# The second expert's first product made by seven quarter products, with the sums for it ordered among the first expert's work

## The chip, the cores and the metric

The kernel runs on one core of a Trainium2 chip. The time is that of the device, in microseconds (us), of one execution; the kernel before was executed three times. The profile is one further look at such an execution, with every instruction's start and duration. TensorE is called PE in it, VectorE DVE, ScalarE ACT, GpSimd POOL, and SP is the engine whose queue issues nearly all transfers here.

## The reference

Causal attention with a forgetting bias, then a mixture of 8 experts whose weights come from a Sinkhorn normalisation over all tokens, then a bilinear layer. There are 1152 tokens (2 x 576) of width 512; an expert is 512 to 1024 to 512.

```python
attn = softmax(q @ k.T / 8 + min(-(cum_i - cum_j), 0), causal)   # 2 batches, 8 heads, 576 x 64
x = (attn @ v) as (1152, 512)
P = exp(x @ w_gate - max)
for _ in range(8):                       # Sinkhorn
    P /= P.sum(1, keepdims=True) + 1e-9
    P /= P.sum(0, keepdims=True) + 1e-9
    P *= 1152 / 8
out = sum_e P[:, e:e+1] * (relu(x @ w1[e]) @ w2[e])
return (out @ w_a) * (out @ w_b) @ w_out
```

## The kernel before

Each float32 matrix is held as two float16 parts, a high one (`hi_of`, on ACT) and the remainder (`lo_of`, on DVE), and each product is three PE products (high x high, high x low, low x high). Weights arrive in `stage` buffers of 1 MB, their scale is found (`sumsq` on ACT, a maximum over partitions, `pow2` on DVE), and `split` writes the two parts into `wun` buffers. Nine token tiles `t` = 0 to 8 go through attention; tile 8 holds the last 64 tokens of both batches.

The program is not written in its final order. Every piece of work is an entry of a graph (`g.add`, with an engine, a cost, keys that it reads and writes, and a rank), and `emit` makes the order of each engine by list scheduling with the costs of the entries. It does so in two parts: entries ahead of the mark `g.cut` are planned and re-ranked first, those behind it are planned after that, on engines that are already taken up to the end of the first part. So on every engine all of the first part stands ahead of all of the second.

The first part is attention and, tile by tile, the gate and expert 0 (`e0_tile`: gate product, two `h_quad` of 48 matmuls with 128 columns, then 24 matmuls with 512 columns into `mb`, L1041 to L1043). `switch` closes the attention buffers and opens those of the experts (`ht`, `sx`, `ts`, `mr`) once all tiles of `xt`, the transposed input of the experts, are there. The last entry of the first part is `w_prep(1, 1, ...)`, load, scale and split of expert 1's `w1`.

The second part begins with `sinkhorn()`: a maximum of the logits (L1144), a transpose and a broadcast on PE (L508, L510), an exponential on ACT (L1148), eight rounds of four DVE operations over rows (L1151 to L1154), one PE product with ones (L1168) and five DVE operations over columns (L1160 to L1164), then nine scalings of `acc` (L1176). Expert 1's first product is `h_plain`: three blocks of 384 tokens, eight columns of weights, 12 matmuls each (L998 to L1000), one eviction by ACT (L1003) and one by DVE (L1004). Experts 2 to 7 use `h_seven`: both factors are cut into quarters, seven products of sums of quarters replace eight, in matmuls of 288 columns (L1393 to L1395), with additions on DVE (L1408), copies on ACT (L1412) and the evictions L1403 and L1404. For it `x_sums` makes four sums of quarters of x once (28 additions on DVE at L1317, eight copies on ACT at L1321, rank 202.5, behind `w_prep(2, 1, ...)`), and `w_sums` makes the sums of the weights for each expert (four subtractions L1351, seven pairs of L358 on ACT and L372 on DVE). All experts end with `y_tile`: per token tile 24 matmuls with 512 columns (L1041 to L1043) into one of two `yb` banks and an eviction into `acc` (L1451).

Of the kernel before, what the change touches and what calls it, by code (L numbers as in the profile page):

```python
# [11 lines left out]
F16 = mybir.dt.float16  # L12
# [40 lines left out]
class Graph:  # L53
# [179 lines left out]
    def emit(self):  # L233
        self.begin()
        self.stale = True
        for seed in SEEDS:
            self.rerank(seed)
        state = self.schedule(0, self.cut)
        order = self.order
        self.schedule(self.cut, None, state)  # L240
        for t, i, k in order + self.order:
            fn = self.ops[i][2]
            (fn[k] if isinstance(fn, tuple) else fn)()
# [3 lines left out]
def forgetting_attention_moe_bilinear_kernel(  # L247
# [22 lines left out]
    KF = FF // 128  # L270
# [3 lines left out]
    NB = NTL // BT  # L274
    BN = BT * 128
# [8 lines left out]
    g = Graph()  # L284
# [18 lines left out]
    stage = [const.tile([128, 2048], F32, name=f"stage{i}") for i in range(2)]  # L303
    units = [const.tile([128, 2, 4, 512], F16, name=f"wun{i}") for i in range(4)]
# [4 lines left out]
    CN = HT // 2  # L309
# [99 lines left out]
    st = [aps.tile([128, 512], F32, name=f"st{i}") for i in range(NST)]  # L409
# [12 lines left out]
    def mbk(m):  # L422
# [11 lines left out]
          w=["clamp"], rank=0)  # L434
# [525 lines left out]
    def frank():  # L960
        fr[0] += 1
        return 1e4 + fr[0]
# [131 lines left out]
    yb = []  # L1094

    def switch():
        att.close()
        bp = ctx.enter_context(tc.tile_pool(name="big", bufs=1))
        for i in range(4, 7):
            units.append(bp.tile([128, 2, 4, 512], F16, name=f"wun{i}"))  # L1100
        big["ht"] = bp.tile([128, 2, KF, NT], F16, name="ht")
        big["sx"] = bp.tile([128, 4, 2, 2, HT], F16, name="sx")
        big["jk"] = bp.tile([128, 1024], F16, name="jk")
        big["mr"] = bp.tile([128, 2048], F32, name="mr")
        for i in range(2):
            big["ts", i] = bp.tile([128, 1024], F32, name=f"ts{i}")
            big["s5", i] = bp.tile([128, CN], F32, name=f"s5_{i}")
            big["w", i] = bp.tile([128, CN], F32, name=f"w22_{i}")
            big["o", i] = big["ts", i][:, 0:DM]
        stage.append(big["mr"])  # L1110
        for i in range(2):
            units.append(stage[i].bitcast(F16).rearrange("p (z c f) -> p z c f", z=2, c=4))
        big["g0"] = big["sx"].rearrange("p i z c t -> p (i z c t)").rearrange("p (z f t) -> p z f t", z=2, f=4)
        yp = ctx.enter_context(tc.tile_pool(name="ps_y", bufs=1, space=PSUM))
        mb.append(yp.tile([128, 512], F32, name="mb2"))
        for i in range(5):
            yb.append(yp.tile([128, 512], F32, name=f"yb{i}"))
# [4 lines left out]
    def hk(z, f, c0=0, c1=NT):  # L1122
# [1 line left out]

    allh = [x for z in range(2) for f in range(KF) for x in hk(z, f)]
    sxk = [("sx", i, z, c) for i in range(4) for z in range(2) for c in range(2)]
    bigk = ([("u", i, z, c) for i in range(4, 7) for z in range(2) for c in range(4)] + [("yb", i) for i in range(5)] + allh + sxk
            + [("o", i) for i in range(2)] + [("a", i) for i in range(2)] + [("s5", i) for i in range(2)] + [("w", i) for i in range(2)]
            + [("st", 2, c) for c in range(4)] + mbk(2) + ["switch"])
    g.add("-", 0, switch, r=attk, w=bigk)  # L1130
# [157 lines left out]
    def h_cols(c0, c1):  # L1288
        return (lambda z, f: big["ht"][:, z, f, c0:c1]), (lambda z, f: hk(z, f, c0, c1))

    def h_plain(e):

        for b in range(NB):
            dst, dkey = h_cols(b * BN, (b + 1) * BN)
            for f in range(KF):
                h_item(e, b * BN, BN, f, dst, dkey)

    def slot(i):
        return (0, 1, 4, 5)[i // 2], 2 * (i % 2)

    def slot_keys(i):
        u, c0 = slot(i)
        return [("u", u, z, c) for z in range(2) for c in (c0, c0 + 1)]

    quad = lambda z, r, t: xt[:, z, 2 * r:2 * r + 2, t * HT:(t + 1) * HT]

    def x_sums():

        rk = 202.5
        sk, uk = [("o", 0), ("a", 0)], [("o", 1), ("a", 1)]  # L1310
        xk = [("xt", t) for t in range(NTL)]
        for c in range(2):
# [28 lines left out]
    def w_sums(e, rank):  # L1341
# [9 lines left out]
            g.add("DVE", 1280, lambda: nc.vector.tensor_tensor(out=out(), in0=a(), in1=b(), op=ALU.subtract), r=r, w=w, rank=rank)  # L1351

        def split(i, src, keys):
            u, c0 = slot(i)
            part = [lambda y=y: units[u][:, y, c0:c0 + 2].rearrange("p c f -> p (c f)") for y in range(2)]
            k = [[("u", u, y, c) for c in (c0, c0 + 1)] for y in range(2)]
            g.add("ACT", 1144, lambda: hi_of(part[0](), src(), sx), r=keys + [("ws", 1, e)], w=k[0], rank=rank)
            g.add("DVE", 1290, lambda: lo_of(nc.vector, part[1](), src(), sx, part[0]()), r=keys + [("ws", 1, e)] + k[0], w=k[1], rank=rank)
# [15 lines left out]
    def h_seven(e):  # L1374
# [7 lines left out]

        def prod(i, j, c, bank, bk, first):
            src, keys, wi = ops[i]
            u, ch0 = slot(wi)

            def mm():
                p = bank()[:, 0:CN]
# [5 lines left out]
                    nc.tensor.matmul(p, lhsT=wh, rhs=xl, start=False, stop=False, skip_group_check=True)  # L1394
                    nc.tensor.matmul(p, lhsT=wl, rhs=xh, start=False, stop=ch == 1, skip_group_check=True)  # L1395

            g.add("PE", 6 * (CN / 2.4 + 2.7), mm, r=keys + slot_keys(wi), w=bk, rank=frank())

        def out(src, bk, f, s_, c):
            c0 = s_ * HT + c * CN  # L1400
# [279 lines left out]
                    m2_prep(wi, pc, 6, prank())  # L1680
                m2_out(wi, x, prank())

    w_prep(1, 1, (4, 5), 150, fine=True, rel=REL_E1)()
    g.cut = len(g.ops)
    early[0] = False
    dense[0] = True
    sinkhorn()
    g.add("PE", 700, set_bits, r=[("xt", t) for t in range(NTL)], w=[("yb", i) for i in range(2, 5)], rank=frank())
    for e in range(1, E):
        last = e == E - 1  # L1690
        if e == 1:
            h_plain(e)
        else:
            h_seven(e)
        w_prep(2, e, (2, 3), prank())()
        if e == 1:
            x_sums()
        if not last:
            w_prep(1, e + 1, (None, None), prank())
        g.add("-", 0, lambda: None, r=hk(0, 0), w=["hold"])  # L1700
# [78 lines left out]
```

## Time and profile before

| what | value |
|---|---|
| executions | 1064.58, 1064.61, 1066.53 us; median 1064.61 |
| span of the profiled execution | 1065.9 us |
| PE busy | 1009.7 us, 95% of the span |
| DVE busy | 716.6 us, 67% |
| ACT busy | 514.8 us, 48% |
| POOL busy | 156.9 us, 15% |
| mean granted PE clock | 0.992 of 2.4 GHz |

The profile gives no time of its own for the profiled execution beside the span from its first to its last instruction; that span is 1.3 us above the median of the three executions. A matmul's duration in it overlaps the next one's, so the spacing of starts is what a matmul costs. DVE and ACT durations overlap by some 0.1 us likewise.

### The profile page before, as it was taken

How to read it: one execution, taken by the hardware profiler on the slowest of the kernel's cores; microseconds unless marked ns; L12 is line 12 of the kernel's file. 1: busy time of each engine (PE TensorE's matmuls, PEld its weight loads, DVE VectorE, ACT ScalarE, POOL GpSimd, SP SyncE). 2: the span in 40 equal slices, each digit the busy share in tenths (PEclk: the TensorE clock that was granted, in tenths of full speed). 3: DMA queues.
4: the chain of work that ended last, by engine and by line, in shares of the span. 5: the costliest groups of instructions: out<-in, count | busy, mean ns of one | idle time of the engine just before them, and what ended most of it. 6: DMA issues, size and time to landing. Idle time of an engine off the chain costs nothing.

```text
span 1065.9 us, 19044 instructions
## 1 busy us (share of the span) xinstructions
PE 1009.7 (95%) x7739; PEld 626.9 (59%) x7739; DVE 716.6 (67%) x1490; ACT 514.8 (48%) x966; POOL 156.9 (15%) x192
## 2 busy tenths in 40 slices
PE   1498999999999999999999999999999999999998
PEld 0476877765546754764774575476477464555445
DVE  7885674149975898796699879578768785444201
ACT  4587477246534644753662664356444344443100
POOL 3977576120000000000000000000000000000000
PEclk9899999999999999999999999999999999999999
DMA  9893951002223125423323340341443652310001
GB/s 240 161 195 78 173 81 23 2 15 76 79 80 117 43 104 173 159 80 119 119 80 121 147 168 41 120 155 43 158 158 110 207 129 79 119 40 1 21 30 40
DMA packets 123063, 108.75 MB, mean 102 GB/s; under 512 B 87632, under 2 KB 100176, under 8 KB 119136
## 3 DMA queue, kind: packets, MB, share of 16 engines
q1 hardware_dynamic: 121920, 107.27, 34.3%
q8 instruction: 60, 0.98, 0.4%
q10 hardware_dynamic: 1056, 0.28, 0.1%
q14 instruction: 27, 0.22, 0.1%
HBM read 75.29 MB, written 18.09 MB: 88 GB/s over the span
## 4 chain that ended last, share of the span: by engine, by line
PE 88%; DVE 6%; DMA 2%; issue 1%; POOL 1%; ACT 1%; SPq 0%; DVEq 0%; POOLq 0%; ACTq 0%
PE yb L1041 10%; PE yb L1042 10%; PE yb L1043 10%; PE yb L1393 4%; PE yb L1395 4%; PE yb L1394 4%; PE mb L1393 3%; PE mb L1394 3%; PE mb L1395 3%; PE yb L1647 2%; PE yb L1648 2%; PE yb L1649 2%; PE yb L1578 2%; PE yb L1579 2%; PE yb L1577 2%; DVE wun L372 2%
## 5 line engine op out<-in xcount | busy, mean ns | idle before, releaser
L1041 PE MATMUL yb<-wun,ht 128*128 128x512 f16 x504 | 191.1, 379 | 0.0
L1042 PE MATMUL yb<-wun,ht 128*128 128x512 f16 x504 | 191.1, 379 | 0.0
L1043 PE MATMUL yb<-wun,ht 128*128 128x512 f16 x504 | 191.1, 379 | 0.0
L372 DVE SCALAR_TENSOR_TENSOR wun<-stage,sc,wun 128x1024 f16<-128x1024 f32 (+1 forms) x66 | 79.7, 1231 | 11.5 <-ACT wun L358 11.5
L1043 PEld LDWEIGHTS <-ht 128*128 128x128 f16 x504 | 49.3, 98 | 59.5
L1393 PE MATMUL yb<-sx,wun 128*128 128x288 f16 x288 | 82.4, 286 | 2.0 <-DVE sc L343 1.1
L1451 DVE SCALAR_TENSOR_TENSOR acc<-yb,pe,acc 128x512 f32<-128x512 f32 x63 | 47.3, 750 | 54.1 <-PE yb L1043 53.1
L1042 PEld LDWEIGHTS <-ht 128*128 128x128 f16 x504 | 49.3, 98 | 57.7 <-issue 0.3
L1041 PEld LDWEIGHTS <-ht 128*128 128x128 f16 x504 | 49.3, 98 | 57.6
L1395 PE MATMUL yb<-sx,wun 128*128 128x288 f16 x288 | 82.4, 286 | 0.0
L1394 PE MATMUL yb<-sx,wun 128*128 128x288 f16 x288 | 82.4, 286 | 0.0
L1394 PEld LDWEIGHTS <-wun 128*128 128x128 f16 x672 | 65.7, 98 | 24.7 <-issue 6.2
L1393 PEld LDWEIGHTS <-wun 128*128 128x128 f16 x672 | 65.7, 98 | 18.4
L1395 PEld LDWEIGHTS <-wun 128*128 128x128 f16 x672 | 65.7, 98 | 16.6
L358 ACT ACTIVATE wun<-stage,sc 128x1024 f16<-128x1024 f32 (+1 forms) x58 | 59.7, 1052 | 29.8 <-DVE sc L343 14.7
L355 ACT ACTIVATE jk<-stage 128x1024 f16<-128x1024 f32 x52 | 54.7, 1052 | 37.5 <-DMA stage<-in_moe_w_dram 37.1
L897 POOL TENSOR_TENSOR pt<-p,pt 128x512 f16<-128x512 f32 (+1 forms) x46 | 55.0, 1198 | 25.3 <-ACT pt L894 19.4
L1403 ACT ACTIVATE ht<-yb 128x288 f16<-128x288 f32 x96 | 38.8, 406 | 40.7 <-PE yb L1395 40.1
L1393 PE MATMUL mb<-xt,wun 128*128 128x288 f16 x192 | 55.0, 286 | 0.0
L1394 PE MATMUL mb<-xt,wun 128*128 128x288 f16 x192 | 55.0, 286 | 0.0
L1395 PE MATMUL mb<-xt,wun 128*128 128x288 f16 x192 | 54.9, 286 | 0.0
L1404 DVE SCALAR_TENSOR_TENSOR ht<-yb,ht 128x288 f16<-128x288 f32 x96 | 43.0, 453 | 17.2 <-ACT ht L1403 16.9
(355 smaller groups left out, 2641.8 us busy)
## 6 DMA issues: line engine op xcount, KB each, us to landing
stage<-in_moe_w_dram SPq DMA_DIRECT2D x26, 1024.0 KB, 5.5
md<-wun SPq DMA_DIRECT2D x15, 1024.0 KB, 3.8
wun<-md SPq DMA_DIRECT2D x11, 1024.0 KB, 5.4
stage<-in_moe_w_dram SPq DMA_DIRECT2D x24, 256.0 KB, 3.9
mr<-in_moe_w_a_dram SPq DMA_DIRECT2D x12, 512.0 KB, 6.0
mr<-in_moe_w_b_dram SPq DMA_DIRECT2D x12, 512.0 KB, 4.0
mr<-in_moe_w_out_dram SPq DMA_DIRECT2D x6, 1024.0 KB, 5.4
stage<-md SPq DMA_DIRECT2D x4, 1024.0 KB, 4.8
```

The lines of the kernel that those rows point to most:

```text
L355: nc.scalar.activation(out, src, AF.Square, accum_out=dst)
L358: nc.scalar.activation(hi, src, AF.Copy, scale=scale)
L372: eng.scalar_tensor_tensor(out=lo, in0=src, scalar=scale, in1=hi, op0=ALU.mult, op1=ALU.subtract)
L897: lambda hi=hi, lo=lo, src=src: nc.gpsimd.tensor_tensor(out=lo, in0=src, in1=hi, op=ALU.subtract)),
L1041: nc.tensor.matmul(pp, lhsT=hh, rhs=wh, start=(f == 0), stop=False)
L1042: nc.tensor.matmul(pp, lhsT=hh, rhs=wl, start=False, stop=False)
L1043: nc.tensor.matmul(pp, lhsT=hl, rhs=wh, start=False, stop=(f == KF - 1))
L1393: nc.tensor.matmul(p, lhsT=wh, rhs=xh, start=first and ch == 0, stop=False, skip_group_check=True)
L1394: nc.tensor.matmul(p, lhsT=wh, rhs=xl, start=False, stop=False, skip_group_check=True)
L1395: nc.tensor.matmul(p, lhsT=wl, rhs=xh, start=False, stop=ch == 1, skip_group_check=True)
L1404: g.add("DVE", 160 + 1.04 * CN, lambda: nc.vector.scalar_tensor_tensor(out=hl(), in0=src(), scalar=0.0, in1=hh(), op0=ALU.max, op1=ALU.sub ...
L1451: g.add("DVE", 663, lambda t=t, z=z: nc.vector.scalar_tensor_tensor(out=acc[:, t], in0=yb[z], scalar=pe[:, t, e:e + 1], in1=acc[:, t], op0 ...
```

## The change

Expert 1's first product becomes `h_seven` too. Its weights' load and scale, `x_sums` and `w_sums(1)` stand between `g.cut` and a new mark `g.cut2`: they are planned together with the first part, with ranks from 1e6 up, which lets everything else of the first part go ahead where both are ready, but they are not re-ranked with it. The plain split of expert 1's `w1` is gone; its scale now uses POOL's reduction over partitions and no PE transposes. The seven weight sums of expert 1 go to `wun` 4, 5, 6 and to a ninth buffer that is a view of `mr`. `h_plain` is gone.

```diff
-        state = self.schedule(0, self.cut)
+        state = self.schedule(0, self.cut2)
         order = self.order
-        self.schedule(self.cut, None, state)
+        self.schedule(self.cut2, None, state)
...
+        units.append(stage[2].bitcast(F16).rearrange("p (z c f) -> p z c f", z=2, c=4))
...
-    def slot(i):
-        return (0, 1, 4, 5)[i // 2], 2 * (i % 2)
+    def slot(e, i):
+        return ((0, 1, 4, 5) if e > 1 else (4, 5, 6, 9))[i // 2], 2 * (i % 2)
...
-    def x_sums():
+    def x_sums(rk):
-        rk = 202.5
...
-    w_prep(1, 1, (4, 5), 150, fine=True, rel=REL_E1)()
     g.cut = len(g.ops)
     early[0] = False
+    w_prep(1, 1, (None, None), 1e6, rel=REL_E1)
+    x_sums(1e6 + 1)
+    w_sums(1, 1e6 + 2)
+    g.cut2 = len(g.ops)
     dense[0] = True
     sinkhorn()
...
     for e in range(1, E):
         last = e == E - 1
+        h_seven(e)
         if e == 1:
-            h_plain(e)
-        else:
-            h_seven(e)
+            g.add("-", 0, lambda: None, w=[("u", 9, z, c) for z in range(2) for c in range(4)] + [("st", 2, c) for c in range(4)])
         w_prep(2, e, (2, 3), prank())()
-        if e == 1:
-            x_sums()
```

In the changed kernel the lines move by a few: L1310 and L1314 are the sums of x and their copies (L1317 and L1321 before), L1344 the subtractions of `w_sums` (L1351), L1386 to L1388 the products of `h_seven` (L1393 to L1395), L1396 and L1397 its evictions (L1403, L1404), L1401 its additions (L1408), L1405 its copies (L1412), L1145 the logits' maximum (L1144), L1149 the exponential (L1148).

DVE at the end of the first expert, before: the last two evictions of tile 7 (L1028 into `h_1`), the logits of tile 8 (L982), and further on the split of expert 1's weights and the first operation of `sinkhorn`.

```order
L1028 SCALAR_TENSOR_TENSOR h_1_80<-mb_84,h_1_80 128x512
L1028 SCALAR_TENSOR_TENSOR h_1_80<-mb_85,h_1_80 128x512
L982 TENSOR_SCALAR logit<-mb_85,isx,sc 128x8
L490 TENSOR_REDUCE sc<-sc 128x1
L1028 SCALAR_TENSOR_TENSOR h_0_79<-mb_85,h_0_79 128x512
...
L372 SCALAR_TENSOR_TENSOR wun_3527<-stage_73,sc,wun_3527 128x512 x4
L372 SCALAR_TENSOR_TENSOR wun_3528<-stage_74,sc,wun_3528 128x512 x3
L1144 TENSOR_REDUCE sc<-logit 128x1
```

The same place now: the sums of x begin right behind tile 7's evictions.

```order
L1028 SCALAR_TENSOR_TENSOR h_1_80<-mb_84,h_1_80 128x512
L1028 SCALAR_TENSOR_TENSOR h_1_80<-mb_85,h_1_80 128x512
L1310 TENSOR_TENSOR ts_3526<-xt 128x576
L1310 TENSOR_TENSOR ts_3529<-xt 128x576
L1310 TENSOR_TENSOR ts_3526<-ts_3526,ts_3529 128x576
L1310 TENSOR_TENSOR ts_3529<-xt 128x576
L982 TENSOR_SCALAR logit<-mb_85,isx,sc 128x8
L490 TENSOR_REDUCE sc<-sc 128x1
L1310 TENSOR_TENSOR sx<-ts_3526,sx 128x576
```

And its end, further down DVE's list: the weight sums and then `sinkhorn` (L1145, L509).

```order
L1344 TENSOR_TENSOR ts_3529<-stage_74 128x1024
L1310 TENSOR_TENSOR sx<-ts_3526,sx 128x576
L1344 TENSOR_TENSOR ts_3526<-stage_74,stage_73 128x1024
L372 SCALAR_TENSOR_TENSOR wun_3521<-ts_3529,sc,wun_3521 128x1024
L372 SCALAR_TENSOR_TENSOR wun_3520<-ts_3526,sc,wun_3520 128x1024
L1344 TENSOR_TENSOR ts_3526<-stage_74,ts_3526 128x1024
L372 SCALAR_TENSOR_TENSOR wun_3521<-ts_3526,sc,wun_3521 128x1024
L1344 TENSOR_TENSOR ts_3526<-stage_73,ts_3526 128x1024
L372 SCALAR_TENSOR_TENSOR mr<-ts_3526,sc,mr 128x1024
L1145 TENSOR_REDUCE sc<-logit 128x1
L509 TENSOR_REDUCE sc<-yb_3536 1x1
L1148 TENSOR_SCALAR sc<-yb_3536 128x1
```

Between the two pieces stand the other 23 sums of x, tile 8's two evictions and three splits of plain quarters; all of it now stands ahead of `sinkhorn`.

PE behind expert 0's last matmuls, before: three matmuls that set bits in the `yb` banks, then the plain product.

```order
L1043 MATMUL mb_84<-wun_78,h_0_79 128x512
L1443 LDWEIGHTS xt
L1443 MATMUL yb_3546<-xt 128x512
...
L998 LDWEIGHTS wun_3527
L998 MATMUL mb_3543<-xt,wun_3527 128x384
```

The same place now: `wun_3519` holds the sums 0 and 1, `wun_3520` the sums 2 and 3, `wun_3521` 4 and 5, `mr` 6; product 1 reads plain x and sum 0, product 5 reads `sx` and sum 3.

```order
L1043 MATMUL mb_84<-wun_78,h_0_79 128x512
L1436 LDWEIGHTS xt
L1436 MATMUL yb_3538<-xt 128x512
...
L1386 MATMUL mb_85<-xt,wun_3519 128x288
...
L1386 MATMUL mb_84<-xt,wun_3519 128x288
...
L1386 MATMUL mb_3535<-sx,wun_3520 128x288
...
L508 MATMUL yb_3536<-id_60,sc 1x128
L1386 LDWEIGHTS wun_3519
```

Product 1 (two banks) and product 5 (twice into one bank), 24 matmuls, stand ahead of `sinkhorn`'s transpose L508; the other 52 of the 56 groups of six matmuls stand behind it, and 36 of the 216 matmuls of `y_tile` stand ahead of the last group.

ACT around `sinkhorn`'s exponential, before: one eviction of `h_plain` (L1003), the sums of squares of expert 1's `w2` (L355), the exponential.

```order
L1321 ACTIVATE sx<-ts_3534 128x576
L355 ACTIVATE jk,sc<-stage_73 128x1024
L1003 ACTIVATE ht<-mb_84 128x384
L1148 ACTIVATE pe<-logit,sc 128x72
L355 ACTIVATE jk,sc<-stage_73 128x1024
```

The same place now.

```order
L1405 ACTIVATE yb_3539<-mb_85 128x288
L355 ACTIVATE jk,sc<-stage_74 128x1024
L1405 ACTIVATE s_1_3530<-mb_3535 128x288
L355 ACTIVATE jk,sc<-stage_74 128x1024
L355 ACTIVATE jk,sc<-stage_73 128x1024
L1149 ACTIVATE pe<-logit,sc 128x72
```

Three of the four sums of squares of `w2` now stand ahead of the exponential; they read `stage_74` and `stage_73`, which `w_sums(1)` reads too.

## Rows read from the trace of the kernel before

**Rows 1.** Page: the chain that ended last, shares by engine
```profile
PE 88%; DVE 6%; DMA 2%; issue 1%; POOL 1%; ACT 1%; SPq 0%; DVEq 0%; POOLq 0%; ACTq 0%
```

**Rows 2.** Stages: window and length; PE, PEld, DVE, ACT, POOL busy; clock, DMA
```profile
220.00:237.90 17.90, 16.98 (x162) 10.91 (x161) 7.59 (x16) 10.11 (x25) 4.83 (x5) 1.00 0.00 1
237.90:287.80 49.90, 48.81 (x307) 30.02 (x306) 47.76 (x134) 27.33 (x51) 3.32 (x4) 1.00 0.25 85
287.80:334.70 46.90, 46.86 (x219) 21.36 (x218) 31.48 (x53) 17.23 (x21) 0.35 (x1) 1.00 0.14 46
334.70:376.00 41.30, 41.30 (x333) 32.46 (x332) 33.74 (x72) 27.63 (x63) 0.91 (x2) 1.00 0.30 102
```

**Rows 3.** Timeline of PE (start, duration): last attention product, last of expert 0, first of expert 1
```profile
214.03 0.20 PE L917 MATMUL xp<-vs,pt 128*64 128x65 f16 x1
...
237.20 0.38 PE L1043 MATMUL mb<-wun,h 128*128 128x512 f16 x1
...
238.07 0.33 PE L998 MATMUL mb<-xt,wun 128*128 128x384 f16 x1
```

**Rows 4.** Tile xt, 195 to 240 us: its last transposing transfer, and time to landing
```profile
L940 SPq DMA_TRANSPOSE xt<-xhl x1: 1232/1232/1232, 217.0 to 217.0; - x1
...
DMA to landing us min/median/max: 3.0/3.0/3.0
```

**Rows 5.** Timeline of DVE, 220 to 312 us (start, duration)
```profile
220.66 0.69 DVE L1028 SCALAR_TENSOR_TENSOR h<-mb,h 128x512 f16<-128x512 f32 x1 [1.99 <-ACT h L1027]
...
240.91 0.21 DVE L1144 TENSOR_REDUCE sc<-logit 128x1 f32<-128x72 f32 x1
...
260.43 0.75 DVE L1317 TENSOR_TENSOR sx<-ts,sx 128x576 f16<-128x576 f32 x1
261.10 0.23 DVE L1160 TENSOR_REDUCE sk<-yb 128x8 f32<-128x72 f32 x1
...
262.16 0.55 DVE L1004 SCALAR_TENSOR_TENSOR ht<-mb,ht 128x384 f16<-128x384 f32 x1
262.63 0.22 DVE L1151 TENSOR_REDUCE sk<-pe 128x9 f32<-128x72 f32 x1
...
263.50 1.28 DVE L372 SCALAR_TENSOR_TENSOR wun<-stage,sc,wun 128x1024 f16<-128x1024 f32 x1
264.69 0.55 DVE L1004 SCALAR_TENSOR_TENSOR ht<-mb,ht 128x384 f16<-128x384 f32 x1
...
294.30 3.65 DVE L1176 TENSOR_SCALAR acc<-acc,pe 128x512 f32<-128x512 f32 x9
...
307.77 1.22 DVE L1351 TENSOR_TENSOR ts<-stage,ts 128x1024 f32<-128x1024 f32 x1
...
310.20 1.28 DVE L372 SCALAR_TENSOR_TENSOR wun<-ts,sc,wun 128x1024 f16<-128x1024 f32 x1 [0.23 <-ACT wun L358]
311.52 1.22 DVE L1351 TENSOR_TENSOR ts<-stage,ts 128x1024 f32<-128x1024 f32 x1
```

**Rows 6.** Timeline of DVE in expert 2's seven products
```profile
374.59 0.81 DVE L1404 SCALAR_TENSOR_TENSOR ht<-yb,ht 128x288 f16<-128x288 f32 x2
375.32 0.45 DVE L1408 TENSOR_TENSOR yb<-yb,s 128x288 f32<-128x288 f32 x1
```

**Rows 7.** Timeline of ACT, a sum of squares; issues from 60 us on (KB, us to landing)
```profile
247.74 1.06 ACT L355 ACTIVATE jk<-stage 128x1024 f16<-128x1024 f32 x1 [0.63 <-DMA stage<-in_moe_w_dram]
...
stage<-in_moe_w_dram SPq DMA_DIRECT2D x8, 1024.0 KB, 5.1
```

**Rows 8.** Stages in attention, columns as in Rows 2
```profile
44.00:48.00 4.00, 0.48 (x10) 0.36 (x10) 3.90 (x7) 1.53 (x3) 4.00 (x5) 0.82 0.66 131
48.00:52.00 4.00, 2.75 (x25) 2.23 (x26) 2.41 (x13) 2.75 (x5) 2.41 (x4) 0.50 1.18 171
52.00:56.00 4.00, 4.00 (x33) 3.49 (x32) 3.14 (x10) 2.47 (x6) 2.50 (x3) 0.50 1.08 231
56.00:60.00 4.00, 4.00 (x74) 3.61 (x71) 3.06 (x9) 3.76 (x9) 2.39 (x3) 0.90 0.87 251
```

More of the change, by code (lines that the diff above doesn't have):

```diff
@@ L1126, in forgetting_attention_moe_bilinear_kernel @@
     sxk = [("sx", i, z, c) for i in range(4) for z in range(2) for c in range(2)]
-    bigk = ([("u", i, z, c) for i in range(4, 7) for z in range(2) for c in range(4)] + [("yb", i) for i in range(5)] + allh + sxk
+    bigk = ([("u", i, z, c) for i in (4, 5, 6, 9) for z in range(2) for c in range(4)] + [("yb", i) for i in range(5)] + allh + sxk
             + [("o", i) for i in range(2)] + [("a", i) for i in range(2)] + [("s5", i) for i in range(2)] + [("w", i) for i in range(2)]
@@ L1289, in h_cols, with slot_keys @@
         return (lambda z, f: big["ht"][:, z, f, c0:c1]), (lambda z, f: hk(z, f, c0, c1))
[L1291 to L1296, printed above, removed]
-    def slot(i):
-        return (0, 1, 4, 5)[i // 2], 2 * (i % 2)
-    def slot_keys(i):
-        u, c0 = slot(i)
+    def slot(e, i):
+        return ((0, 1, 4, 5) if e > 1 else (4, 5, 6, 9))[i // 2], 2 * (i % 2)
+    def slot_keys(e, i):
+        u, c0 = slot(e, i)
         return [("u", u, z, c) for z in range(2) for c in (c0, c0 + 1)]
     quad = lambda z, r, t: xt[:, z, 2 * r:2 * r + 2, t * HT:(t + 1) * HT]
-    def x_sums():
-        rk = 202.5
+    def x_sums(rk):
         sk, uk = [("o", 0), ("a", 0)], [("o", 1), ("a", 1)]
@@ L1353, in split @@
         def split(i, src, keys):
-            u, c0 = slot(i)
+            u, c0 = slot(e, i)
             part = [lambda y=y: units[u][:, y, c0:c0 + 2].rearrange("p c f -> p (c f)") for y in range(2)]
@@ L1384, in prod @@
             src, keys, wi = ops[i]
-            u, ch0 = slot(wi)
+            u, ch0 = slot(e, wi)
             def mm():
@@ L1395, in mm @@
                     nc.tensor.matmul(p, lhsT=wl, rhs=xh, start=False, stop=ch == 1, skip_group_check=True)
-            g.add("PE", 6 * (CN / 2.4 + 2.7), mm, r=keys + slot_keys(wi), w=bk, rank=frank())
+            g.add("PE", 6 * (CN / 2.4 + 2.7), mm, r=keys + slot_keys(e, wi), w=bk, rank=frank())
         def out(src, bk, f, s_, c):
```

## The prediction

> **What bounds the kernel now.** I read the chain that ended last first: PE carries 88% of it [rows 1]. Then the busy times by stage [rows 2]. The stage of expert 1's first product, 237.9 to 287.8, takes 49.9 us with PE busy 48.8; its y tiles (287.8 to 334.7) take 46.9 with PE busy throughout; expert 2's seven products (334.7 to 376.0) take 41.3, all PE. So PE sets the pace in all three, and from expert 2 on there is no gap into which a delay could be absorbed: what the program is late by at the end of expert 1's y tiles, it is late by at its end. DVE is the engine to watch: 47.8 of 49.9 us busy in expert 1's first product, but only 7.6 of 17.9 us in the last stretch of expert 0, 220.0 to 237.9 [rows 2]. The change moves work from the full stretch into the other one.
>
> **What is removed.** Plain product against seven products: 49.9 us against 41.3 [rows 2], 8.6 us less PE time if nothing waits. A group of six matmuls costs 41.3 / 56 = 0.74 us, a matmul of the y tiles 46.9 / 216 = 0.217 us. The scale of expert 1's weights loses its two PE transposes, worth about 1 us of expert 0's end; as PE waits right behind it (below), I count nothing for it.
>
> **Where the sums can start.** They read all of `xt`, so they wait for the last tile. Its transfer is issued at 217.0 and lands 3.0 later [rows 4], at 220.0. In DVE's new list they stand behind tile 7's second eviction, which starts at 220.66 [rows 5] and gives DVE free at 221.3. In the order of both kernels two whole tiles of expert 0 stand on PE behind the last attention product. That product starts at 214.03 and expert 0 ends at 237.4 [rows 3], so the sums have some 16 us of cover and no more.
>
> **How long the sums take.** A sum of x costs 0.67 (260.43 to 261.10), a split of 1024 columns 1.19 (263.50 to 264.69) [rows 5]. Four sums bring DVE to 224.0. Then tile 8's logits stand in its list; their PE work comes half way between 214.03 and 237.4, at about 225.7, and the first copy on ACT stands behind four sums of squares of 1.06 each [rows 7]: I let DVE go on at 226.5. Up to the sum of weights that product 5 needs there stand 24 sums (16.1), two evictions of 0.6 (1.2), three splits (3.6), two subtractions of 1.22 less an overlap of 0.08 (2.3), two splits (2.4), small operations (0.5), and eight places where DVE waits a little for ACT's copy (1.2 together, an estimate). That is 27.3, so 253.8. PE has done product 1's twelve matmuls by 239.5 (238.07 [rows 3] plus 1.5) and stands until then: **14.3 us of wait**, more than the 8.6 gained.
>
> **What is queued behind it.** Two more weight sums follow, each a subtraction, a copy on ACT, a remainder: 307.77 to 311.52 is one such link, 3.75 [rows 5]. So DVE comes to the first operation of `sinkhorn` at 261.3; before it was at 240.91 [rows 5]. PE's list has `sinkhorn`'s transpose behind 24 matmuls, so PE does product 5 (1.5 us) and stands again to 261.5, though sums for other products are there. Then ACT: three sums of squares of `w2` now stand ahead of the exponential. Their buffer is read last by the last subtraction, 257.6 to 258.7; a load of 1 MB takes 5.1 and the sum of squares 1.06 [rows 7], so the exponential comes at 265.0 and DVE's first round of `sinkhorn` at **266.0**, with half a us for the exponential and the crossings.
>
> **DVE's list from there.** Up to the last but one addition (the one that frees the products of the last column block) the order has 28 evictions of 0.365 (10.2) and 14 additions of 0.37 (5.2) [rows 6], eight rounds of 0.87 over rows (262.63 to 263.50) and 1.06 over columns (261.10 to 262.16), 7.0 and 8.5, nine scalings of `acc` (3.6), four splits of `w2` (4.8) [rows 5] and small ones (0.7): **40.0 us without a single wait**, to 306.0. PE's groups need 52 x 0.74 = 38.5 from 261.5, so DVE is the longer list, and PE, three of whose seven products wait for a DVE addition, follows it. Behind that addition PE has three groups (2.2) and 192 of the 216 matmuls of the y tiles (41.7) left; the other 24 fit before. The y tiles end at 349.9; before they ended at 334.7 [rows 2]. That is 15.2 us late.
>
> **Unknowns.** DVE's waits within the 40 us: below by nothing, above by a crossing and a group of products in each of the eight rounds, 8 x (0.74 + 0.23) = 7.8, the 0.23 being the wait for ACT at 310.20 [rows 5]. In expert 1's stage before, with the same rounds, DVE was idle 2.1 us [rows 2]; the new list crosses more often, and I take 3. PE's clock: after 44 to 48, with PE busy 0.48 of 4 us, the granted clock was 0.50 in 48 to 56, that is 1.2 GHz, and 0.90 in 56 to 60 [rows 8]. The waits here are longer, so the first groups after 261.5 run at the half level; that stretch of 8 us at 0.50 costs PE 4 us, between nothing and that on the path, and I take 1, since DVE starts its rounds only at 266.0.
>
> The Trainium skill (TensorE: Matmul & The Clock Gate, "What's actually happening") says that the throttled clock is the default state and that activity releases it; by that alone the restart would cost the whole 4 us and the sum would be 1087. The rows agree on the fall and the return (0.82, 0.50, 0.50, 0.90), and it is the order of DVE's list that makes me count less.
>
> The first part is planned anew, since eight loads, sums of squares and splits left it. Its first 40 us are nearly the same order; later rows change places. A hole such as 44 to 56 cost PE some 8 us (3.5 of idle time, then half the clock) [rows 8]; one may close or open. I take nothing, plus or minus 8.
>
> **The sum.** 15.2 + 3 + 1 = 19.2 us. The profiled span, 1065.9, is 1.3 above the median; I add to the median: 1064.6 + 19.2 = **1084**.
>
> **Rivals.**
> First, the wait ends at the first products. If DVE's interleaving costs PE nothing after 253.8, PE does the 54 groups left (39.8) and the y tiles (46.9) to 340.5: 5.8 late, 1070. For it: expert 1's plain product lived with DVE 96% busy. Against it: it needs DVE's 40.0 us to fit, which begin 12 us after PE could go on.
> Second, the two engines run in step: all 7.8 us of crossings and the 4 us of clock, 15.2 + 11.8 = 27, 1092, and more if a hole opens in the first part. For it: both lists are in order and each holds the other's inputs.
> Third, the other side: the sums are hidden, as the first part's free DVE time suggests (10.3 us idle in 220.0 to 237.9), and the 8.6 us are gained: 1056. It decides at the transfer of the last tile: that would have to land about 14 us sooner against PE's end of expert 0 for product 5, and over 20 for `sinkhorn`, so before 206. Both orders leave the last attention product ahead of the same two tiles, which speaks against it.
> Fourth, the new plan of the first part wins back what the sums lose. It takes 19 us, two holes like 44 to 56 closed; no change then, and some gain if the waits come out short too.
>
> **How the numbers follow.** The forecast (1076 to 1092 as its own range) 0.58, the first rival 0.15, the second from 1092 on 0.17, gain by the third or the fourth 0.06, no change 0.04. The range 1070 to 1093 leaves out the upper half of the second rival (0.09) and the last two (0.10). What a measurement of this kernel can tell from no change is about 0.2%, 2 us: faster 0.06, same 0.04, slower 0.90.
>
> **What would show it.** In the changed profile: the transfer of the last tile still some 17 us ahead of expert 0's end on PE; PE idle for 18 to 22 us between then and `sinkhorn`'s transpose, in two pieces, the first ended by DVE's split into the buffer of sum 3, the second by the logits' maximum; that maximum some 24 us behind expert 0's end, where it was 3.5; ACT's exponential behind a sum of squares that waits for a load; the granted clock at 0.5 after the wait; DVE over 90% busy for 40 us; expert 1's y tiles ending 17 to 21 us later against expert 0's end, and the stages from expert 2 on unchanged in length. I am wrong if the sums start well before expert 0's last two tiles, if DVE's list is not what PE waits for in expert 1, or if the first part's length moves by more than 8 us.

## The result, and the profile after

The changed kernel takes 1076.6 us (median of 4, 1075.8 to 1077.6) against 1064.6 us of the kernel before, a ratio of 1.0111 with a 95% interval of 1.0097 to 1.0125. A later set on another chip gave 1.0113 (1.0094 to 1.0133). It is 12 us slower; 1084 was forecast, 1070 to 1093 the range.

The chain that ended last has more of DVE in it than before, 8% against 6% [rows 1]:

```profile
PE 87%; DVE 8%; issue 2%; POOL 2%; DMA 1%; ACT 1%; SPq 0%; POOLq 0%; DVEq 0%; ACTq 0%
```

The stages, in the columns of [rows 2]: the last stretch of expert 0; PE's standing; expert 1's products from 258.4 on; its y tiles; expert 2's products.

```profile
212.30:229.70 17.40, 17.02 (x175) 11.28 (x173) 13.34 (x24) 11.82 (x18) 0.38 (x1) 1.00 0.04 7
229.70:258.40 28.70, 7.85 (x38) 4.38 (x37) 23.44 (x28) 12.00 (x18) 0.00 (x0) 0.58 0.22 74
258.40:307.50 49.10, 47.42 (x359) 35.04 (x359) 44.64 (x151) 26.43 (x60) 1.60 (x2) 1.00 0.12 44
307.50:346.40 38.90, 38.90 (x183) 17.63 (x182) 19.68 (x26) 15.90 (x19) 0.35 (x1) 1.00 0.15 55
346.40:387.70 41.30, 41.30 (x333) 32.47 (x332) 33.75 (x73) 27.54 (x63) 0.91 (x2) 1.00 0.31 102
```

The loss is in the second row: 28.7 us in which PE is busy for 7.9, at a granted clock of 0.58. Expert 2's products take 41.3 as before. PE's waits between 225 and 320 us (tile and line that waited, releaser, us in all, times, longest):

```profile
PE mb L1386 <- ACT wun L358: 14.8, 1, 14.8
PE mb L1386 <- ACT s L1405: 5.3, 1, 5.3
PE yb L1386 <- DVE yb L1401: 1.6, 2, 1.1
PE mb L1388 <- DVE wun L372: 0.7, 1, 0.7
```

PE's timeline at the same places as [rows 3]: last attention product, last matmul of expert 0, then the first product behind each wait, `sinkhorn`'s transpose (L508) with the products behind it, and the place from which PE runs on:

```profile
207.38 0.20 PE L917 MATMUL xp<-vs,pt 128*64 128x65 f16 x1
...
229.50 0.38 PE L1043 MATMUL mb<-wun,h 128*128 128x512 f16 x1
229.72 0.81 PE L1436 MATMUL yb<-xt 128*128 128x512 f16 x3
...
246.85 0.42 PE L1386 MATMUL mb<-sx,wun 128*128 128x288 f16 x1 [14.85 <-ACT wun L358]
...
254.66 0.40 PE L1386 MATMUL mb<-sx,wun 128*128 128x288 f16 x1 [5.35 <-ACT s L1405]
...
256.05 0.42 PE L508 MATMUL yb<-id,sc 128*1 128x128 f32 x1
256.26 0.45 PE L1386 MATMUL mb<-xt,wun 128*128 128x288 f16 x1
256.50 0.45 PE L1387 MATMUL mb<-xt,wun 128*128 128x288 f16 x1
...
258.35 0.30 PE L1386 MATMUL yb<-sx,wun 128*128 128x288 f16 x1
...
346.39 0.29 PE L1386 MATMUL mb<-sx,wun 128*128 128x288 f16 x1
```

DVE's timeline: tile 7's second eviction and the first sums of x right behind it, two remainders (the second is that for sum 3), the last split, the logits' maximum, the first row sum of `sinkhorn`, the last addition but one of the first product. In [rows 5] the maximum stands at 240.91, 3.5 us behind expert 0's end; here it is 25.8 us behind it.

```profile
214.01 0.69 DVE L1028 SCALAR_TENSOR_TENSOR h<-mb,h 128x512 f16<-128x512 f32 x1 [1.99 <-ACT h L1027]
214.61 1.42 DVE L1310 TENSOR_TENSOR ts<-xt 128x576 f32<-128x576 f16 x2
...
245.53 2.58 DVE L372 SCALAR_TENSOR_TENSOR wun<-ts,sc,wun 128x1024 f16<-128x1024 f32 x2
...
254.34 1.28 DVE L372 SCALAR_TENSOR_TENSOR mr<-ts,sc,mr 128x1024 f16<-128x1024 f32 x1 [1.22 <-ACT mr L358]
255.54 0.22 DVE L1145 TENSOR_REDUCE sc<-logit 128x1 f32<-128x72 f32 x1
...
259.87 0.23 DVE L1152 TENSOR_REDUCE sk<-pe 128x9 f32<-128x72 f32 x1
...
301.09 0.46 DVE L1401 TENSOR_TENSOR yb<-yb,s 128x288 f32<-128x288 f32 x1
```

Two points cut the program into three parts: the first matmul behind expert 0 (229.72 here) and the first product of expert 2 (346.39), which is the end of expert 1's y tiles. The table gives them for the traces below (of old_order_late_prep only expert 0's end is read, in the text); the third part is the span less the second point.

| kernel | expert 0 ended | expert 1 took | the rest | span |
|---|---|---|---|---|
| before, first trace | 237.42 | 97.5 | 731.0 | 1065.9 |
| before, second trace | 236.16 | 97.5 | 729.0 | 1062.6 |
| changed | 229.72 | 116.7 | 727.5 | 1073.9 |
| changed, second trace | 229.36 | 116.8 | 728.4 | 1074.6 |
| plain_new_plan | 230.72 | 96.0 | 728.8 | 1055.5 |
| old_plan_sums | 236.54 | 123.0 | 728.2 | 1087.7 |
| w_first | 230.68 | 117.1 | 730.5 | 1078.3 |
| busy_wait | 231.03 | 116.9 | 728.7 | 1076.6 |
| no_x_sums | 230.05 | 100.7 | 728.6 | 1059.3 |
| half_x_sums_pool | 242.24 | 112.6 | 727.4 | 1082.3 |
| sinkhorn_first | 231.07 | 129.3 | 728.3 | 1088.7 |

Between the two second traces: expert 0 ends 6.8 earlier, expert 1 takes 19.3 more, the rest 0.5 less, together 12.0, the difference of their spans. So two terms of opposite sign: a shorter first part and a longer expert 1.

### The profile page after: what moved, and what is told of

It is laid out like the page before. It is cut to its first block, busy times and chain, and to the rows that moved or that the text cites. A ratio compares the mean times of both kernels' runs of the same rounds, so it can differ in the third digit from the quotient of the medians.

```text
span 1073.9 us, 19153 instructions
## 1 busy us (share of the span) xinstructions
PE 1003.0 (93%) x7784; PEld 628.9 (59%) x7784; DVE 731.2 (68%) x1514; ACT 528.0 (49%) x989; POOL 148.1 (14%) x186
## 4 chain that ended last, share of the span: by engine, by line
PE 87%; DVE 8%; issue 2%; POOL 2%; DMA 1%; ACT 1%; SPq 0%; POOLq 0%; DVEq 0%; ACTq 0%
PE yb L1041 10%; PE yb L1043 10%; PE yb L1042 10%; PE yb L1386 5%; PE yb L1388 5%; PE yb L1387 5%; PE mb L1386 4%; PE mb L1387 4%; PE mb L1388 4%; PE yb L1640 2%; PE yb L1641 2%; PE yb L1642 2%; PE yb L1571 2%; PE yb L1572 2%; PE yb L1570 2%; DVE wun L372 2%
## 5 line engine op out<-in xcount | busy, mean ns | idle before, releaser
L1386 PE MATMUL yb<-sx,wun 128*128 128x288 f16 x336 | 96.1, 286 | 3.3 <-DVE yb L1401 2.2
L1386 PEld LDWEIGHTS <-wun 128*128 128x128 f16 x768 | 75.6, 98 | 36.2 <-ACT wun L358 15.2
L1388 PE MATMUL yb<-sx,wun 128*128 128x288 f16 x336 | 96.1, 286 | 0.0
L1387 PE MATMUL yb<-sx,wun 128*128 128x288 f16 x336 | 96.1, 286 | 0.0
L1387 PEld LDWEIGHTS <-wun 128*128 128x128 f16 x768 | 75.3, 98 | 31.5 <-issue 10.3
L1388 PEld LDWEIGHTS <-wun 128*128 128x128 f16 x768 | 75.4, 98 | 20.4 <-DVE wun L372 1.2
L372 DVE SCALAR_TENSOR_TENSOR wun<-stage,sc,wun 128x1024 f16<-128x1024 f32 (+1 forms) x62 | 76.0, 1244 | 10.7 <-ACT wun L358 10.6
L1444 DVE SCALAR_TENSOR_TENSOR acc<-yb,pe,acc 128x512 f32<-128x512 f32 x63 | 47.3, 750 | 52.6 <-PE yb L1043 51.6
L355 ACT ACTIVATE jk<-stage 128x1024 f16<-128x1024 f32 x56 | 59.0, 1053 | 33.9 <-DMA stage<-in_moe_w_dram 33.5
L1396 ACT ACTIVATE ht<-yb 128x288 f16<-128x288 f32 x112 | 45.4, 407 | 52.2 <-PE yb L1388 51.4
L1386 PE MATMUL mb<-xt,wun 128*128 128x288 f16 x224 | 64.4, 287 | 0.0
L1387 PE MATMUL mb<-xt,wun 128*128 128x288 f16 x224 | 64.4, 287 | 0.0
L1388 PE MATMUL mb<-xt,wun 128*128 128x288 f16 x224 | 64.4, 287 | 0.0
L1397 DVE SCALAR_TENSOR_TENSOR ht<-yb,ht 128x288 f16<-128x288 f32 x112 | 50.2, 453 | 17.7 <-ACT ht L1396 17.2
```

Source lines behind the costliest of these rows:

```text
L355: nc.scalar.activation(out, src, AF.Square, accum_out=dst)
L372: eng.scalar_tensor_tensor(out=lo, in0=src, scalar=scale, in1=hi, op0=ALU.mult, op1=ALU.subtract)
L1386: nc.tensor.matmul(p, lhsT=wh, rhs=xh, start=first and ch == 0, stop=False, skip_group_check=True)
L1397: g.add("DVE", 160 + 1.04 * CN, lambda: nc.vector.scalar_tensor_tensor(out=hl(), in0=src(), scalar=0.0, in1=hh(), op0=ALU.max, op1=ALU.sub ...
L1444: g.add("DVE", 663, lambda t=t, z=z: nc.vector.scalar_tensor_tensor(out=acc[:, t], in0=yb[z], scalar=pe[:, t, e:e + 1], in1=acc[:, t], op0 ...
```

## The experiments

The theory behind the forecast: DVE's serial list of sums, which cannot start before the last tile of x, keeps PE standing behind expert 0. Its rivals: the loss lies in the half clock after the wait, or in DVE and PE holding each other from `sinkhorn` on, or only in the first wait of 14.8; and the gain of the first part belongs to one execution or to work that left it. Ratios below are to the kernel before on the same chip, whose median was 1066.1, 1066.2 and 1065.5 us in the three sets.

### The plan without the sums

```diff
-    w_prep(1, 1, (4, 5), 150, fine=True, rel=REL_E1)()
     g.cut = len(g.ops)
     early[0] = False
+    w_prep(1, 1, (4, 5), 1e6, rel=REL_E1)()
+    g.cut2 = len(g.ops)
...
-        state = self.schedule(0, self.cut)
+        state = self.schedule(0, self.cut2)
...
-        self.schedule(self.cut, None, state)
+        self.schedule(self.cut2, None, state)
```

> The changed kernel's first part (the same order on PE up to expert 0's last matmul), but expert 1 keeps its plain product; no sums. Its weights are loaded and split at the end of the first part, in pieces of 1024 columns. If the shorter first part comes from the new plan alone: expert 0 ends on PE near 229.7 again (237.4 before), the plain product starts without a wait, since its eight splits fit between 224 and 231, expert 1's y tiles end some 97 us later, and the time is 1064.6 - 7.8 = 1057, between 1054 and 1060. If the gain belongs to one execution only, or to the sums that stand in the list: 1064.

Measured: 1058.1 us, ratio 0.9931 (0.9917 to 0.9944). Expert 0 ended at 230.7, and between 200 and 330 us PE waited 0.4 us in all. The gain is there without the sums, and this kernel beats both. Expert 1 took 96.0, 1.5 less than before.

### The sums without the plan

```diff
-    g.cut = len(g.ops)
-    early[0] = False
-    w_prep(1, 1, (None, None), 1e6, rel=REL_E1)
+    w_prep(1, 1, (4, 5), 150, fine=True, rel=REL_E1)()
+    g.cut = len(g.ops)
+    early[0] = False
     x_sums(1e6 + 1)
```

> The other half: the first part planned as before (expert 1's weights are loaded, scaled and split in it as before, these splits are then overwritten), with the seven products and the sums of the changed kernel behind it. If plan and sums are two independent terms: expert 0 ends near 237.4 as before, its end to the end of expert 1's y tiles takes 116.8 as in the changed kernel, up to 3 more as DVE has eight small remainders among the sums, and the time is 1064.6 + 19.4 = 1084, between 1081 and 1088. If the plan is not what the first part gained by: 1077.

One of the small remainders is made by GpSimd, which writes the scaled weights back into a quarter of their buffer, so expert 1's sums take that quarter scaled twice; the instructions are the same. Measured: 1090.1 us, ratio 1.0229 (1.0215 to 1.0243), 24 above before. Expert 0 ended at 236.5, as under the old plan, and expert 1 took 123.0, 6.2 more than in the changed kernel where up to 3 were allowed: seven small remainders stand in one piece among the sums.

```profile
235.21 7.59 DVE L372 SCALAR_TENSOR_TENSOR wun<-stage,sc,wun 128x512 f16<-128x512 f32 x7
...
268.18 0.22 DVE L1145 TENSOR_REDUCE sc<-logit 128x1 f32<-128x72 f32 x1
```

The maximum stands 31.6 us behind expert 0's end instead of 25.8. What is put into DVE's list ahead of it comes out as PE's standing. So some 6 of the 24 us are these remainders, which the changed kernel does not have; without them the two halves of the change, -8 and +24, would add up to some 10, near its 12.

### The order of the sums

```diff
-    x_sums(1e6 + 1)
-    w_sums(1, 1e6 + 2)
+    w_sums(1, 1e6 + 1)
+    x_sums(1e6 + 2)
```

> The changed kernel with the sums of the weights written ahead of the sums of x, nothing else. They need no tile of x, so some of them fill DVE's idle time between the last attention product and the last tile of x (5.9 us of waits between 207.6 and 214.6), but the sums of x that the second product waits for stand later in the list. If the whole of DVE's list of sums up to sinkhorn sets the end: sinkhorn starts 2 to 4 us sooner against expert 0's end and the time is 1073 to 1075. If the first wait, that of the second product for sum 0 and its weights, sets the end: it ends near 238 instead of 246.9, and the time is near 1067.

Measured: 1078.2 us, ratio 1.0117 (1.0103 to 1.0131), no different from the changed kernel's 1.0111. Both numbers missed. The first wait did end near 238, and it gained nothing; PE's rows that waited:

```profile
237.95 0.40 PE L1386 MATMUL mb<-sx,wun 128*128 128x288 f16 x1 [4.99 <-ACT sx L1314]
...
248.62 0.40 PE L1386 MATMUL mb<-sx,wun 128*128 128x288 f16 x1 [9.23 <-ACT sx L1314]
...
256.49 0.40 PE L1386 MATMUL mb<-sx,wun 128*128 128x288 f16 x1 [6.44 <-ACT s L1405]
```

So the first wait does not set the end. Nor did the idle time fill: only one subtraction went ahead of tile 7's second eviction, since the splits wait for the scale, and DVE's maximum came 26.2 us behind expert 0's end (256.84 less 230.68), against 25.8. This order within the list was worth nothing; the list is as long as before.

### A busy PE in place of the wait

```diff
-            nc.tensor.matmul(yb[i], lhsT=xt[:, 0, 0, 0:128], rhs=xt[:, 0, 0, 0:512], start=True, stop=True)
+            for _ in range(30):
+                nc.tensor.matmul(yb[i], lhsT=xt[:, 0, 0, 0:128], rhs=xt[:, 0, 0, 0:512], start=True, stop=True)
```

> The changed kernel with 87 more matmuls of 128x512 on PE ahead of expert 1's first product (they write banks that are overwritten), 87 x 0.216 = 18.8 us of work in place of the wait of 14.9 and part of the one of 5.4 behind it. PE is then idle for some 3 us only before 254.7, so the granted clock should stay at 1.00 there instead of 0.50. If the half level costs nothing on the path, since DVE's list sets the end: 1076.6, within 1. If the restart at the half level costs what its stretch of 12.4 us with 5.6 busy suggests: 2.8 to 4 us less, 1073 to 1074.

Measured: 1078.1 us, ratio 1.0112 (1.0098 to 1.0126), the changed kernel's own. The granted clock in the changed kernel, and in this one:

```profile
229.70:246.00 16.30, 2.30 (x16) 1.37 (x14) 15.92 (x21) 5.52 (x8) 0.00 (x0) 0.65 0.00 0
246.00:258.40 12.40, 5.55 (x22) 3.01 (x23) 7.52 (x8) 6.48 (x11) 0.00 (x0) 0.50 0.50 170
258.40:262.00 3.60, 3.60 (x31) 2.89 (x31) 2.50 (x10) 3.02 (x7) 0.35 (x1) 1.00 0.01 2
```

```profile
246.00:252.00 6.00, 6.00 (x35) 3.23 (x34) 4.73 (x5) 2.46 (x3) 0.00 (x0) 1.00 0.08 9
252.00:255.80 3.80, 0.82 (x7) 0.51 (x6) 2.55 (x3) 1.33 (x2) 0.00 (x0) 1.00 0.88 273
255.80:260.00 4.20, 3.77 (x18) 2.26 (x18) 1.71 (x4) 3.27 (x9) 0.00 (x0) 0.64 0.68 240
```

With the clock at 1.00 to 255.8 expert 1 takes 116.9, without it 116.7: ahead of `sinkhorn`'s transpose the half level is spent on products that have time to spare, and it costs nothing there. Behind PE's second wait (3.1 us) and the transpose this run has a half level of its own; the matmuls start 0.24 us apart as in the changed kernel (0.12 at the full level):

```profile
257.12 0.37 PE L508 MATMUL yb<-id,sc 128*1 128x128 f32 x1 [0.27 <-DVE sc L1145]
257.29 0.44 PE L1386 MATMUL mb<-xt,wun 128*128 128x288 f16 x1
257.53 0.44 PE L1387 MATMUL mb<-xt,wun 128*128 128x288 f16 x1
```

So the run does not take that piece away, and does not price it. Six such matmuls and the broadcast stand there on PE in the changed kernel (256.26 to 258.35); by the spacings they cost some 0.7 to 1 us more than at the full level.

### Without the sums of x

```diff
+            if rk >= 1e6:
+                for i in range(4):
+                    split(i, X(0, i % 2, i // 2), xk)
+                continue
```

> The changed kernel with the 20 additions and subtractions of x left out for expert 1: the four operands are plain quarters of x, copied and subtracted as the sums were (expert 1's product is not the reference's). 20 x 0.73 = 14.6 us less on DVE ahead of sinkhorn; PE's work is the same. If DVE's list up to sinkhorn and behind it sets the end, as in the forecast: the first operation of sinkhorn stands some 11 to 12 us behind expert 0's end instead of 26, and the time is 12.0 - 14.5, so 2 to 3 us below the kernel before (1062). If from sinkhorn on PE and DVE hold each other, or the half clock does, whenever they start: the gain is well under 10, a time of 1068 or more.

Measured: 1061.2 us, ratio 0.9963 (0.9949 to 0.9976), by the ratios 4 below before and 16 below the changed kernel; expert 1 takes 16.0 less. That is a little more than DVE's 14.6, since the eight remainders that are left read float16 quarters and take 0.46 instead of 0.76. The maximum stands 8.9 us behind expert 0's end (238.98 less 230.05) instead of 25.8. Of PE's waits ahead of the transpose, 14.8 and 5.3, one of 5.0 is left: the sums of x are the cause of most of the standing. Expert 1 still takes 100.7, more than the 96.0 of the plain product under the same plan.

### Half of the sums on GpSimd

```diff
+            pool = rk >= 1e6 and c == 1
+            S, U = [(lambda i=i, pool=pool: big["tp", i] if pool else big["ts", i][:, 0:HT]) for i in range(2)]
...
+                if pool and w[0][0] == "tp":
+                    g.add("POOL", 1350, lambda: nc.gpsimd.tensor_tensor(out=out(), in0=a(), in1=b(), op=op), r=r, w=w, rank=rk)
...
```

> The changed kernel with the ten sums of the second half of the channels of x on GpSimd, in two buffers of their own; their splits stay on ACT and DVE. All is computed. DVE loses 10 x 0.73 = 7.3 us ahead of sinkhorn. GpSimd's ten at 1.2 to 1.4 us each beside it end near 230, ahead of DVE's list. By DVE's list: 7 us less than the changed kernel, some 5 above the kernel before (1070). If GpSimd and DVE slow each other while both add, or the hand-over costs as much as the sums: 1074 to 1077.

Measured: 1083.2 us, ratio 1.0172 (1.0146 to 1.0197), slower than the changed kernel and past both expectations. Expert 1 did gain 4.1 (112.6), but expert 0 ended at 242.2, 12 later. DVE and GpSimd while both add (tile `tp` is GpSimd's):

```profile
216.49 2.61 DVE L1315 TENSOR_TENSOR ts<-xt 128x576 f32<-128x576 f16 x2
219.13 1.85 DVE L1315 TENSOR_TENSOR ts<-ts,ts 128x576 f32<-128x576 f32 x1
...
228.82 0.15 DVE L334 TENSOR_SCALAR sc<-sc 128x1 f32<-128x1 f32 x1 [4.50 <-POOL sc L497]
...
238.10 0.69 DVE L1028 SCALAR_TENSOR_TENSOR h<-mb,h 128x512 f16<-128x512 f32 x1 [5.56 <-ACT h L1027]
```

```profile
220.44 1.67 POOL L1313 TENSOR_TENSOR tp<-xt 128x576 f32<-128x576 f16 x1
228.41 0.38 POOL L497 PARTITION_ALL_REDUCE sc<-sc  x1 [6.30 <-issue]
235.49 1.39 POOL L1313 TENSOR_TENSOR tp<-tp,tp 128x576 f32<-128x576 f32 x1 [6.70 <-issue]
```

A sum of 0.76 on DVE takes 1.85 beside GpSimd's. And the reduction for the scale of expert 1's weights now stands among GpSimd's sums, with 6.3 us ahead of it (5.4 of them after its input was ready, at 222.99) and 6.7 behind it in which GpSimd does nothing that the trace names; DVE's scale waits for it, and ACT's copy of a late sum holds up the evictions of expert 0's last tile.

### Sinkhorn first

```diff
+    sinkhorn()
     x_sums(1e6 + 1)
     w_sums(1, 1e6 + 2)
     g.cut2 = len(g.ops)
     dense[0] = True
-    sinkhorn()
```

> The changed kernel with sinkhorn written ahead of the sums and planned with the first part: its eight rounds (15.5 us of DVE) stand among the sums, and its matmuls ahead of expert 1's first product. The list ahead of product 5 grows by 15.5, less the crossings that the sums now fill; the list behind it shrinks to some 30 us, less than PE's 40 of products, so PE would run without a wait from product 5 on. By DVE's list: product 5's operands come at 262 to 265 instead of 248, the y tiles of expert 1 end near 351 instead of 346.4, 1081, 4 above the changed kernel. If the late start of sinkhorn (its exponential behind ACT's sums of squares) is what costs: below the changed kernel, 1073 or less.

Measured: 1089.8 us, ratio 1.0228 (1.0205 to 1.0252), slower than the changed kernel as the list theory said, by 12 instead of 4. Product 5 started at 261.90, close to what was expected; then the second half of it waited 5.2 us for ACT's copy of the first, which stands behind ACT's last split, the wait that the changed kernel has too. What PE did from there on (two windows up to the end of the y tiles, less 0.8 us), and the rows around it:

```profile
271.60:320.00 48.40, 48.40 (x351) 35.40 (x351) 37.19 (x76) 36.45 (x74) 0.70 (x2) 0.95 0.19 65
320.00:359.60 39.60, 39.60 (x188) 18.20 (x187) 10.73 (x20) 8.06 (x13) 0.35 (x1) 1.00 0.17 54
```

```profile
271.60 0.40 PE L1386 MATMUL mb<-sx,wun 128*128 128x288 f16 x1 [5.17 <-ACT s L1405]
...
360.39 0.29 PE L1386 MATMUL mb<-xt,wun 128*128 128x288 f16 x1
```

This is the run that decides on the second half of the forecast. `sinkhorn` and the scalings of `acc` are out of DVE's list here, DVE is busy 37 of 48 us, and PE never waits. Yet it needs 88.8 us from 271.60 to expert 2, for 54 groups of 0.74, 216 matmuls of 0.217 (86.9 together) and some 2 us at the half level of the clock. In the changed kernel PE needs 88.0 from 258.35 to 346.39, where DVE was busy 44.6 of 49.1: 51 groups, 216 matmuls and `sinkhorn`'s 16 small ones (1.4) are 86.0, and PE waited 1.6 for two of DVE's additions. So nearly all of the time is PE's own list; DVE's, which is almost as long, adds 1.6.

### Both kernels again, and the old order without the work

The first two are unchanged. The third moves expert 1's sums of squares, scale and splits behind everything else of the first part and keeps the old order of the rest:

```diff
         order = self.order
+        late = [x for x in order if self.w0 <= x[1] < self.cut and not self.ops[x[1]][7]]
+        order = [x for x in order if x not in late] + late
         self.schedule(self.cut, None, state)
...
+    g.w0 = len(g.ops)
     w_prep(1, 1, (4, 5), 150, fine=True, rel=REL_E1)()
```

> The kernel before, unchanged, for a second trace. The first trace has a span of 1065.9, while other executions of it have spans of 1062.3 to 1065.1. If its first part is as long as the order makes it in every execution: expert 0's last matmul within 1 us of 237.4, and the two spells at half clock (near 50 and near 106) are there again. If they belonged to one execution: expert 0 ends near 231, as under the new plan.

> The changed kernel, unchanged, with more rounds and a second trace: 12 above the kernel before, within 1.5, expert 0's last matmul between 229.7 and 231 and expert 1's y tiles 116.7 behind it.

> The kernel before with its own order, from which expert 1's sums of squares, scale and splits (not the eight loads) are taken and put behind everything else of the first part; plain product. Read by expert 0's end on PE alone, since expert 1 then starts late (8 sums of squares at 0.65, the scale and 16 small splits come behind expert 0: some 10 to 12 us, a time near 1070). If the first part got shorter because that work left ACT and DVE: expert 0 ends near 231 with the old order too. If it is the new order that made it shorter: 236 to 237, less the 1.3 of the scale's two transposes.

Measured: before again 1064.4 us, expert 0's last matmul at 235.94, 1.3 from the first trace, a little more than the 1 us allowed. The spell at half clock near 106 is there again:

```profile
100.00:104.00 4.00, 0.89 (x15) 0.55 (x13) 3.76 (x9) 0.62 (x2) 3.29 (x6) 0.90 0.60 115
104.00:108.00 4.00, 3.67 (x34) 3.64 (x35) 1.65 (x10) 0.00 (x0) 1.10 (x6) 0.50 1.11 119
108.00:112.00 4.00, 4.00 (x54) 3.79 (x52) 2.31 (x10) 2.30 (x4) 1.86 (x4) 0.75 0.95 187
```

The changed kernel in the first two of these windows, and in the window in which the first trace of before had its other spell [rows 8]:

```profile
100.00:104.00 4.00, 4.00 (x32) 2.08 (x31) 3.79 (x13) 1.09 (x2) 3.39 (x7) 1.00 0.92 176
104.00:108.00 4.00, 4.00 (x70) 3.87 (x67) 2.18 (x11) 1.35 (x3) 1.77 (x5) 1.00 1.17 135
...
48.00:52.00 4.00, 2.15 (x32) 1.64 (x30) 3.43 (x12) 3.80 (x8) 3.69 (x5) 1.00 0.75 147
```

Before again needs 15.0 us of PE busy at a clock of 0.83 in 100 to 120, the changed kernel 19.3 at 1.00. So that spell belongs to the order, not to one execution. The one near 50 is only lessened: over 40 to 60 the clock is 0.74 in both traces of before, 1.00 and 0.91 in those of the changed kernel. The changed kernel again: 1076.4 us, ratio 1.0113, expert 0 ended at 229.36, 0.3 ahead of the range, and expert 1 took 116.8. The old order with the work moved away: 1080.7 us, since expert 1 starts late, and later than foreseen (1070); but expert 0's last matmul is at 235.22, 0.7 sooner than in before again, and the last attention product at 212.04 against 212.77. Taking the work out of ACT's and DVE's lists brings less than 1 us; the other 6 are the new order's.

## Why the prediction was right or wrong

The direction and the place were right. What expert 1 takes was forecast to grow by 19.2 and grew by 19.2 in the first traces and 19.3 in the second, but that agreement is luck: a wrong step behind `sinkhorn`'s transpose made up for what the sum had missed ahead of it.

**The start and the length of the list.** These held to about 1 us each. The last tile's transfer was issued at 210.37, 19.3 us ahead of expert 0's end, where it stood 20.4 ahead before [rows 3, 4]: the cover is 1.1 shorter than the sum had it. The first sum started 7.2 us behind the last attention product (7.3 forecast), the remainder for sum 3 ended 40.7 behind it (39.8), the maximum started 48.2 behind it (47.3). The first wait was 14.8 (14.3); what ended it was ACT's copy for sum 3, and DVE's remainder added 0.7. The step that PE's list has `sinkhorn`'s transpose in order, and stands for it, held too. I had not named ACT's copy of product 5, behind ACT's split for the last weight sum; PE stood 5.3 for it, but nearly all of that it would have stood for the maximum anyway. The transpose started at 256.05, 26.3 behind expert 0's end, where 24.1 was forecast (261.5 less 237.4): 1.1 from the shorter cover, 0.9 from the longer list, 0.3 from product 5.

**DVE's list from there.** This step failed. I wrote that DVE's 40.0 us without a wait are the longer list and that PE follows it, added 3 for DVE's waits and 1 for the clock, and came to 92.4 us from the transpose to the end of the y tiles. PE's own groups and y tiles were 38.5 and 46.9 of it, so I had DVE and the clock hold PE for 7.0. Measured are 90.3 (256.05 to 346.39). Nearly all of it is PE's own list, with `sinkhorn`'s products (2 us in all) that I had left out of it; the clock costs about 1, and PE waited 1.6 for two of DVE's additions, at 282.96 and 293.72, not for the last but one, which was to hold it. With `sinkhorn` taken out of DVE's list (sinkhorn_first) PE had no wait there and took as long for its own list. So the sum was 2.2 too small ahead of the transpose and 2.1 too large behind it, and the total came out right by these two errors. What decides is DVE's list ahead of `sinkhorn`: where the maximum came 5.8 later against expert 0's end (old_plan_sums), 4.2 sooner (half_x_sums_pool) or 16.9 sooner (no_x_sums), expert 1 took 6.3 more, 4.1 less and 16.0 less.

**The clock.** It fell to 0.50 in the wait and was back at 1.00 from 258.4. I took 1 of 0 to 4 for the restart, and the spacings behind the transpose give about that. The Trainium skill (TensorE: Matmul & The Clock Gate, "What's actually happening") says that the throttled clock is the default and that activity releases it; the rows agree. The whole 4 us were not to be paid, since most of the stretch at the half level lies ahead of the transpose, where busy_wait shows that it costs nothing; in sinkhorn_first, where PE's products are what the end waits for, the restart costs some 2 us.

**The first part.** The term that was mis-sized: I took nothing, plus or minus 8, for the new plan. It brought 6.8 (7.7 against the first trace of before). I had named the mechanism, a hole that closes, and the hole at 104 to 112 did close, but I had read only the first 40 us of the new order and so had no ground to choose a sign. With it the forecast would have been 1084 - 6.8 = 1077.

**The rivals.** The first had PE run on from the first wait without another one; it stood again ahead of the transpose, but behind it PE went at its own pace, as this rival said. The second, both engines in step, would have shown in PE's waits, and these are 1.6 us in all. The gain of 8.6 by the plain count is not there: in no_x_sums, with most of the sums gone, expert 1 still takes 3 us longer than before. The fourth rival, the new plan wins back what the sums lose, came true by a third. I had given it only the change as a whole; as a term by itself it was the better part of the change, and plain_new_plan shows what it is worth alone, 8 us.

What stays open: why the search over ranks finds the better order when eight loads, eight sums of squares and the splits are missing from its list. old_order_late_prep shows that it is the order; whether the same search would find it with other seeds was not tried.

## What to carry to other kernels

A change that re-plans a schedule is two changes: run the plan without the edit and the edit without the plan before judging either; here they were -8 and +24 (6 of these the experiment's own), and the better kernel was the one that the change did not aim at. Work moved into a stretch where its engine looks idle has to be measured against the time from its last input to the first use of its result: the sums had 15 us there (214.61 to 229.72), and the list that they stand in took 41 (214.61 to 255.54). Where two in-order engines run side by side, add up both lists in full, the small operations too, before one is called the pace; here they were within 2 us of each other. And where a total agrees, compare its parts: this one agreed by two errors.

## What the hardware showed that I had not expected

DVE and GpSimd adding from SBUF at the same time slowed each other: 0.76 became 1.85 on DVE, and GpSimd's ten sums took 1.27 to 2.26. The Trainium skill (SBUF — State Buffer, "Who interferes with whom") says that a DVE instruction with two SBUF inputs contends with a GpSimd instruction that reads SBUF; the rows agree.

A reduction over partitions on GpSimd among additions had 6.3 us ahead of it and 6.7 behind it without any named cause. In the changed kernel the reduction for the same scale starts at 219.33, 0.1 us behind the end of the DVE operation that it needs, after 9 us in which GpSimd was idle. The Trainium skill (GPSIMD Engine Reference, "2.1 Instruction dispatch") gives about 6 us for the first call of freshly loaded code, without an instruction in the profile. The size is near that of both pauses, which stand at the two changes between the kinds of operation; that code was loaded in them is not shown by any run here.

Two traces of the same kernel before differ by 3.3 us in span (1065.9 and 1062.6), 1.3 of it in the first part and 2.0 from expert 2 on. A term of 7 us read against one trace carries that much doubt.
